# First head group's scores in float32 from raw q and k, its probabilities copied by VectorE, and seven expert matmuls in every unit

## The chip, the cores and the metric

The kernel runs on one core of a Trainium2 chip. The metric is the device time of one execution in microseconds (us). Five engines work side by side, each through its own list of instructions in order: TensorE (PE, matmuls and their weight loads), VectorE (DVE), ScalarE (ACT), GpSimd (POOL) and SyncE (SP), whose list here issues nearly all the DMAs. They wait for each other at semaphores. Matmul results land in PSUM, in eight banks.

## The reference, cut to what matters

Attention with a window of 128 positions and four sink positions for 2 batches, 8 heads, 768 positions and 64 dimensions; its output, 1536 rows of 512, goes through a mixture of 8 experts (hidden width 1024) and then through a dense layer pair (hidden width 2048).

```python
scores = scale * np.matmul(q, k.transpose(0, 1, 3, 2))
keep = is_sink | in_window
scores = np.where(keep, scores, -1e9)
a = np.exp(scores - max); a = a / (sum + 1e-9)
x = np.matmul(a, v)                  # then rows of 512
h = np.maximum(x @ w1[e], 0.0)       # for each expert e
out += P[:, e:e+1] * (h @ w2[e])     # P: balanced gate
```

## The kernel before

**Stages.** `phase_a` computes the attention and, in its gaps, the first chunk of the first expert; `phase_b` does the rest of that chunk and all other chunks. Most products are made in three fp32r passes: each operand is split into a high part (cast by ACT) and a low part (operand minus high part, by POOL or DVE), and the passes are low x high, high x low, high x high.

**Units.** The attention is cut into 4 head groups (batch and half of the sequence) of 4 head pairs each, and each pair `n` into three units `l`, one for 128 rows of queries. Unit `u = 3n + l`. The first group is u = 0 to 11 (n < HP = 4). The score block of a unit is 128, 256 or 288 columns wide in the first and third group (672 in all for a pair) and 288 in the others. Both heads of a pair stand in the two halves of the 128 partitions.

**The loop** (`phase_a`, one turn for each u) issues in this order: the scores of unit u + 2 (`att_qk`, PE); the exponential of unit u + 1 (`att_exp`, ACT); from the second group on the sum, reciprocal and normalisation of unit u (`att_sum`, `att_recip`, `att_norm`, DVE); the masked maximum of unit u + 2 (`att_max`, DVE); a part of `att_x` for the pair before (the output's high part on ACT, its low part `xl` on DVE or POOL); `evac()`, which empties the PSUM bank of every expert group that is complete; a number of steps of the filler; the transposes of unit u (`att_transpose`, PE) and their copy out of PSUM (`att_copy`, ACT: pT, and skT in units with l = 2); in units with l = 0 the product with v for the pair before (`att_av`, PE).

**The first group** is normalised late: `late_recip` builds reciprocals of the row sums and spreads them over 384 columns (DVE), `late_rows` transposes these (L300, PE) and copies them out (L301, DVE), and `att_x` multiplies the output with them (L393, DVE).

**The filler** steps through the 25 groups of `first_groups`, 12 matmuls each: for each of four blocks of 384 rows four groups of `mm1` (384 columns, L593) and three of `mm2` (512 columns, L618), the last three of `mm2` being issued by `phase_b`. A thirteenth step closes a group and opens the next. A block of rows may be worked on only when its attention is complete: `ready` is 0 up to u = 12, 1 up to u = 25, 2 up to u = 37, then 3. Each unit takes up to `MMS[l]` steps and stops at a group's end (`not self.done`). All these groups use the two banks of `ps_mm`. Scores of odd units of the first group use these banks too (`mmtile`).

**The loads.** `att_load_qk` issues q and k of a pair, `att_load_v` its v. The raw tile of pair n + 3 is loaded when that of n + 2 has been split, into the only buffer of `attraw` (pair 1 has a tile of its own among pT's).

**The end.** `phase_b` takes its weight tiles from the space that the attention gives back, loads the next chunk's weights, runs the filler to its end (with `units`, the splits of the next chunk's weights, between its groups) and then begins the next chunk (`plain`, L751).

Of the kernel before, what the change touches and what calls it, by code (L numbers as in the profile page):

```python
# [10 lines left out]
F32 = mybir.dt.float32  # L11
# [13 lines left out]
MMS = (4, 8, 8)  # L25
# [23 lines left out]
class Kernel:  # L49
# [119 lines left out]
    def att_load_qk(self, n, cut=None):  # L169
        g, hp = divmod(n, HP)  # L170
        b, half = divmod(g, 2)
        if n == 1:
            raw = self.attp.tile([128, 2 * S], F32, tag="pth", name="raw1")
        else:
            raw = self.attraw.tile([128, QKW[1]], F32, tag="raw", name="raw")
        cuts = [0, QKW[half]] if cut is None else [0, cut, QKW[half]]
        for i, j in zip(cuts, cuts[1:]):
            self.nc.sync.dma_start(out=raw[:, i:j], in_=self.qkv[half][b, hp][:, i:j])
        self.raw[n] = raw
# [10 lines left out]
    def att_split_qk(self, n, part):  # L190
        nc = self.nc
        half = (n // HP) % 2
        if part == 0:
            self.qk[n] = tuple(
                self.att2.tile([128, QKW[1]], F32R, tag="qk" + t, name="qk" + t) for t in "hl"
            )
        hi, lo = self.qk[n]
        raw = self.raw[n]
        if n == 0:

            def cut(t):
                if part == 3:
                    return t[:, 2 * QW : QKW[half]]
                t = t[:, 0 : 2 * QW].rearrange("p (j c) -> p j c", c=QW)
                return t[:, :, 128 * part : 128 * part + 128]

        else:
            m = QW + 256 if half == 0 else QW + WB

            def cut(t):  # L210
                return t[:, 0:m] if part == 0 else t[:, m : QKW[half]]

        nc.scalar.activation(out=cut(hi), in_=cut(raw), func=AF.Copy)  # L213
        nc.gpsimd.tensor_tensor(  # L214
            out=cut(lo), in0=cut(raw), in1=cut(hi.bitcast(F32)), op=ALU.subtract
        )
# [15 lines left out]
    def att_qk(self, u):  # L232
        nc = self.nc
        n, l, g, hp, half, off, wd, mask, tt = self.unit(u)
        hi, lo = self.qk[n]
# [4 lines left out]
        for a in range(2):  # L240
# [5 lines left out]
            for m, (x, y) in enumerate(((lo, hi), (hi, lo), (hi, hi))):  # L246
                nc.tensor.matmul(
                    out=ps[:, 0:wd],
                    lhsT=x[r, l * 128 : (l + 1) * 128],
                    rhs=y[r, QW + off : QW + off + wd],  # L250
                    start=(m == 0),
                    stop=(m == 2),
                )
# [93 lines left out]
    def att_copy(self, u):  # L347
# [4 lines left out]
        if l == 0:  # L352
            self.pT[n] = self.attp.tile([128, 2, 768], F32, tag="pth", name="pT")
        nc.scalar.activation(
            out=self.pT[n][:, :, o : o + w], in_=self.ptp.pop(u)[:, :, 0:w], func=AF.Copy
        )
        if l == 2:
            w = 128 if half == 0 else QW
            nc.scalar.activation(out=self.skT[0:64, 0:w], in_=self.skp[:, 0:w], func=AF.Copy)
# [673 lines left out]
    def run(self):  # L1033
# [18 lines left out]
        if True:  # L1052
            with tc.manual_schedule():
# [3 lines left out]
                with ExitStack() as actx:  # L1057
                    self.wraw = self.pool(actx, "wraw0")
                    self.att = self.pool(actx, "att")
                    self.attraw = self.pool(actx, "attraw")  # L1060
# [123 lines left out]
    def phase_a(self, gen):  # L1184
# [6 lines left out]
        for part in range(4):  # L1191
            self.att_split_qk(0, part)
        self.att_split_qk(1, 0)
# [9 lines left out]
        self.att_split_qk(1, 1)  # L1203
        self.att_load_qk(2)
        self.att_load_v(1)
        fill = self.filler(gen)
        at = next(fill)
        for u in range(U + 2):
# [9 lines left out]
            if u == 3 * HP - 1:  # L1218
                self.att_transpose(u)
                self.att_copy(u)  # L1220
# [12 lines left out]
            if l == 1 and n and not now:  # L1233
                steps = self.att_x(n - 1)
                next(steps, None)
            if l == 2 and 0 < n < HP:
                next(steps, None)
                next(steps, None)
            if late and l == 2:
                self.late_recip(n)  # L1240
            self.evac()
            if u < 3 * HP - 1:
# [4 lines left out]
            for _ in range(MMS[l]):  # L1247
                ready = 1 if 3 * HP < u < 6 * HP else (u - 2) // (3 * HP)
                if at is not None and at < ready * QW and not self.done:
# [10 lines left out]
            if l == 1 and n + 2 < N:  # L1260
# [235 lines left out]
```

## Time and profile before

| | us |
|---|---|
| median of 3 runs | 1396.65 (1395.65 to 1397.15) |
| profiled execution, its own time | 1395.19 |
| span of that execution, first to last instruction | 1393.0 |
| PE busy | 1369.5 |
| DVE busy | 948.7 |
| POOL busy | 512.9 |
| ACT busy | 462.4 |

How to read what follows: busy times are of one profiled execution. A row of the order of time begins with the start and the duration in us, then engine, line, operation, output <- input, the number of instructions merged in the row (xN) and, in brackets, how long the engine was idle before it and on what it had waited. A matmul in float32 appears as two instructions.

### The profile page before, as it was taken

What the parts mean: (1) busy time and instruction counts of PE and PEld (TensorE: products, weight loads), DVE (VectorE), ACT (ScalarE), POOL (GpSimd) and SP (SyncE); (2) the same over time, 40 slices, a digit from 0 to 9 for tenths busy, and PEclk for the clock granted to TensorE, in tenths of its full rate; (3) what the DMA queues carried; (4) which work ended last, traced back from release to release, by engine and by line L of the source; (5) the groups of instructions that cost most, each with busy time, mean ns of one, the idle gap of its engine ahead of it and who ended that gap; (6) DMA issues with size and microseconds to landing.
All of it is one profiled execution on the core that took longest, in us unless ns stands there. A gap on an engine that the chain in (4) does not pass through costs nothing.

```text
span 1393.0 us, 18988 instructions
## 1 busy us (share of the span) xinstructions
PE 1369.5 (98%) x7129; PEld 1148.4 (82%) x7129; DVE 948.7 (68%) x1868; ACT 462.4 (33%) x1033; POOL 512.9 (37%) x452
## 2 busy tenths in 40 slices
PE   7899999999999999999999999999999999999998
PEld 5566888888888888888888888888888888888887
DVE  5778348987867777777777777675454557876564
ACT  8767323322222222222222322222222234443331
POOL 6422116543432334244333434343333035543310
PEclk9999999999999999999999999999999999999999
DMA  5323200222223232322323132330102010211101
GB/s 168 97 87 91 76 15 17 76 68 95 80 91 106 76 106 66 109 84 91 105 63 121 54 121 69 106 106 32 61 31 61 31 57 5 76 44 63 46 24 71
DMA packets 61146, 102.53 MB, mean 74 GB/s; under 512 B 3956, under 2 KB 43252, under 8 KB 60788
## 3 DMA queue, kind: packets, MB, share of 16 engines
q1 hardware_dynamic: 61040, 101.22, 22.5%
q8 instruction: 58, 0.95, 0.3%
q14 instruction: 44, 0.36, 0.1%
q10 hardware_dynamic: 4, 0.00, 0.0%
HBM read 89.67 MB, written 11.53 MB: 73 GB/s over the span
## 4 chain that ended last, share of the span: by engine, by line
PE 78%; DVE 0%; issue 0%; DVEq 0%
PE mm L902 41%; PE mm L751 36%; PE mm L919 0%; DVE acc L642 0%; DVE acc L638 0%; DVE raw L567 0%; DVE tx L811 0%; DVE raw L554 0%; DVE tu L811 0%; DVE acc L635 0%; DVE raw L559 0%; DVE raw L563 0%; DVEq L642 0%; DVE m L571 0%; DVEq L811 0%
## 5 line engine op out<-in xcount | busy, mean ns | idle before, releaser
L902 PE MATMUL mm<-w2h,hh 128*128 128x512 f32 (+1 forms) x916 | 357.0, 390 | 0.0
L902 PE MATMUL mm<-w2l,hh 128*128 128x512 f32 (+1 forms) x916 | 355.9, 389 | 0.0
L902 PE MATMUL mm<-w2h,hl 128*128 128x512 f32 (+1 forms) x916 | 355.7, 388 | 0.0
L471 POOL TENSOR_TENSOR w2l<-raw,w2h 128x512 fp32r<-128x512 f32 x76 | 118.4, 1558 | 383.7 <-ACT w2h L470 381.8
L642 DVE SCALAR_TENSOR_TENSOR acc<-mm,P,acc 128x512 f32<-128x512 f32 x168 | 125.6, 748 | 135.5 <-PE mm L902 134.1
L902 PEld LDWEIGHTS mm<-w2h,hl 128*128 128x128 f32 x916 | 172.0, 188 | 35.8
L902 PEld LDWEIGHTS mm<-w2h,hh 128*128 128x128 f32 x916 | 172.1, 188 | 34.6
L902 PEld LDWEIGHTS mm<-w2l,hh 128*128 128x128 f32 x916 | 172.1, 188 | 34.4
L514 POOL TENSOR_TENSOR raw<-raw 128x256 f32<-128x256 f32 x136 | 125.8, 929 | 9.0 <-DMA raw<-w 1.1
L471 POOL TENSOR_TENSOR s0l<-raw,s0h 128x512 fp32r<-128x512 f32 (+1 forms) x36 | 45.5, 1265 | 199.0 <-ACT s0h L470 199.0
L719 ACT ACTIVATE hh<-tx 128x512 fp32r<-128x512 f32 (+1 forms) x112 | 58.9, 525 | 130.0 <-DVE tx L811 129.5
L811 DVE TENSOR_TENSOR tx<-mm,tu 128x512 f32<-128x512 f32 (+1 forms) x136 | 75.6, 556 | 21.5 <-PE mm L751 17.4
L811 DVE TENSOR_TENSOR tx<-mm,tx 128x512 f32<-128x512 f32 (+1 forms) x68 | 37.9, 557 | 57.0 <-PE mm L751 55.7
L729 DVE SCALAR_TENSOR_TENSOR hl<-tx,hh 128x512 fp32r<-128x512 f32 (+1 forms) x112 | 70.0, 625 | 9.8 <-ACT hh L719 9.8
L825 ACT ACTIVATE tx<-mm 128x512 f32<-128x512 f32 x34 | 20.4, 599 | 159.7 <-PE mm L751 157.8
L214 POOL TENSOR_TENSOR qkl<-raw,qkh 128x672 fp32r<-128x672 f32 (+5 forms) x34 | 42.7, 1279 | 74.2 <-ACT qkh L213 44.4
L635 DVE TENSOR_TENSOR acc<-mm,acc 128x512 f32<-128x512 f32 (+1 forms) x49 | 33.2, 677 | 50.9 <-PE mm L902 50.5
L719 ACT ACTIVATE hh<-mm 128x512 fp32r<-128x512 f32 (+1 forms) x68 | 34.2, 502 | 99.4 <-PE mm L751 99.4
L825 ACT ACTIVATE txs<-mm 128x256 f32<-128x256 f32 x34 | 13.0, 382 | 151.3 <-PE mm L751 151.3
L471 POOL TENSOR_TENSOR a0l<-raw,a0h 128x512 fp32r<-128x512 f32 (+1 forms) x38 | 43.8, 1171 | 51.1 <-ACT a0h L470 51.1
L751 PE MATMUL mm<-xl,a1h 128*128 128x512 f32 (+1 forms) x172 | 60.3, 350 | 0.0
L751 PE MATMUL mm<-xl,a0h 128*128 128x512 f32 (+1 forms) x172 | 59.8, 348 | 0.0
(262 smaller groups left out, 3202.8 us busy)
## 6 DMA issues: line engine op xcount, KB each, us to landing
raw<-w SPq DMA_DIRECT2D x110, 512.0 KB, 3.5
raw<-win SPq DMA_DIRECT2D x16, 512.0 KB, 4.0
w<-m SPq DMA_DIRECT2D x32, 256.0 KB, 4.7
raw<-wout SPq DMA_DIRECT2D x16, 512.0 KB, 4.1
raw<-qkv SPq DMA_DIRECT2D x8, 624.0 KB, 3.8
raw<-qkv SPq DMA_DIRECT2D x7, 464.0 KB, 3.4
out<-acc SPq DMA_DIRECT2D x11, 256.0 KB, 2.0
wraw<-w SPq DMA_DIRECT2D x2, 1024.0 KB, 6.5
```

The lines of the kernel that those rows point to most:

```text
L214: nc.gpsimd.tensor_tensor(out=cut(lo), in0=cut(raw), in1=cut(hi.bitcast(F32)), op=ALU.subtract)
L471: self.nc.gpsimd.tensor_tensor(out=lo, in0=src, in1=hi.bitcast(F32), op=ALU.subtract)
L514: self.nc.gpsimd.tensor_tensor(out=o, in0=x, in1=y, op=op)
L635: nc.vector.tensor_tensor(out=a, in0=ps, in1=a, op=ALU.add)
L642: nc.vector.scalar_tensor_tensor(out=a, in0=ps, scalar=self.P[:, ti, e : e + 1], in1=a, op0=ALU.mult, op1=ALU.add)
L719: nc.scalar.activation(out=hh, in_=src, func=AF.Relu)
L729: nc.vector.scalar_tensor_tensor(out=hl, in0=src, scalar=0.0, in1=hh.bitcast(F32), op0=ALU.max, op1=ALU.subtract,)
L751: self.nc.tensor.matmul(out=ps, lhsT=w[:, kc], rhs=x[:, kc], start=start and k == 0, stop=(k == n - 1), skip_group_check=True,)
L811: nc.vector.tensor_tensor(out=v[name], in0=v[a], in1=v[b], op=ALU.add)
L825: nc.scalar.activation(out=v["s"], in_=v["a"], func=AF.Copy)
L902: self.nc.tensor.matmul(out=ps[:, d], lhsT=x[:, f, s], rhs=w[:, f, d], start=(n == 0), stop=(n == 11),)
```

## The change

The first head group's scores are made in one float32 matmul for each head from the raw tiles, without a split of q and k; pairs 0 to 3 get raw tiles of their own, all issued at the start together with the load of pair 4, and `attraw` gets two buffers. In the first group `att_copy` runs on VectorE. `late_recip` moves ahead of the two `att_x` steps, and the transposes of unit 11 move back from before the exponential to their regular place. Each unit takes seven steps of the filler, whatever l, and goes on across a group's end.

```diff
-MMS = (4, 8, 8)
+MMS = 7
...
     def att_load_qk(self, n, cut=None):
-        if n == 1:
-            raw = self.attp.tile([128, 2 * S], F32, tag="pth", name="raw1")
+        if n < HP:
+            raw = self.att.tile([128, QKW[0]], F32, name=f"raw{n}")
...
     def att_qk(self, u):
-        hi, lo = self.qk[n]
+        if n < HP:
+            terms = ((self.raw[n],) * 2,)
+        else:
+            hi, lo = self.qk[n]
+            terms = (lo, hi), (hi, lo), (hi, hi)
...
-            for m, (x, y) in enumerate(((lo, hi), (hi, lo), (hi, hi))):
+            for m, (x, y) in enumerate(terms):
...
-                    stop=(m == 2),
+                    stop=(m == len(terms) - 1),
...
     def att_copy(self, u):
-        nc.scalar.activation(
-            out=self.pT[n][:, :, o : o + w], in_=self.ptp.pop(u)[:, :, 0:w], func=AF.Copy
-        )
+        jobs = [(self.pT[n][:, :, o : o + w], self.ptp.pop(u)[:, :, 0:w])]
         if l == 2:
             w = 128 if half == 0 else QW
-            nc.scalar.activation(out=self.skT[0:64, 0:w], in_=self.skp[:, 0:w], func=AF.Copy)
+            jobs.append((self.skT[0:64, 0:w], self.skp[:, 0:w]))
+        for out, src in jobs:
+            if n < HP:
+                nc.vector.tensor_copy(out=out, in_=src)
+            else:
+                nc.scalar.activation(out=out, in_=src, func=AF.Copy)
...
-                    self.attraw = self.pool(actx, "attraw")
+                    self.attraw = self.pool(actx, "attraw", 2)
...
     def phase_a(self, gen):
-        for part in range(4):
-            self.att_split_qk(0, part)
-        self.att_split_qk(1, 0)
...
         self.att_exp(0)
-        self.att_split_qk(1, 1)
         self.att_load_qk(2)
         self.att_load_v(1)
+        for n in (HP - 1, HP):
+            self.att_load_qk(n)
...
-            if u == 3 * HP - 1:
-                self.att_transpose(u)
-                self.att_copy(u)
...
+            if late and l == 2:
+                self.late_recip(n)
             if l == 2 and 0 < n < HP:
                 next(steps, None)
                 next(steps, None)
-            if late and l == 2:
-                self.late_recip(n)
             self.evac()
-            if u < 3 * HP - 1:
+            if late:
                 self.att_transpose(u)
                 self.att_copy(u)
...
-            for _ in range(MMS[l]):
+            for _ in range(MMS):
                 ready = 1 if 3 * HP < u < 6 * HP else (u - 2) // (3 * HP)
-                if at is not None and at < ready * QW and not self.done:
+                if at is not None and at < ready * QW:
                     at = next(fill, None)
...
-            if l == 1 and n + 2 < N:
+            if l == 1 and HP <= n + 2 < N:
                 self.att_split_qk(n + 2, 0)
                 self.att_split_qk(n + 2, 1)
```

## Rows read from the trace of the kernel before

**Rows 1.** The page, busy time of an engine and its share of the span
```profile
PE 1369.5 (98%) x7129; PEld 1148.4 (82%) x7129; DVE 948.7 (68%) x1868; ACT 462.4 (33%) x1033; POOL 512.9 (37%) x452
```

**Rows 2.** Stretches: length, busy time of each engine (instructions), granted clock, DMA
```profile
12.73:19.35 6.62, 6.62 (x55) 4.76 (x55) 4.06 (x20) 6.49 (x22) 4.75 (x5) 1.00 0.36 108
16.72:22.31 5.59, 5.36 (x50) 3.73 (x49) 3.73 (x17) 5.46 (x19) 4.21 (x4) 1.00 0.31 97
...
28.00:32.00 4.00, 4.00 (x27) 2.62 (x26) 0.69 (x2) 3.65 (x13) 3.48 (x3) 0.58 0.39 130
...
38.00:42.00 4.00, 3.97 (x24) 2.69 (x24) 3.44 (x17) 0.00 (x0) 0.00 (x0) 0.61 0.61 179
...
59.65:69.82 10.17, 8.88 (x65) 6.33 (x65) 9.08 (x42) 7.58 (x24) 3.43 (x3) 1.00 0.25 77
```

**Rows 3.** Waits of PE, 0 to 46 and 42 to 185: total, times, longest
```profile
PE mm L300 <- DVE acc L286: 3.2, 1, 3.2
PE ptp L331 <- ACT p L272: 2.1, 2, 1.9
...
PE ptp L331 <- DVE p L318: 6.4, 7, 1.3
```

**Rows 4.** Groups of ACT from 12.73 to 19.35: count, busy, mean ns
```profile
L354 ACT ACTIVATE pT<-ptp 128x512 f32<-128x512 f32 x2 | 1.2, 585 | 0.1
...
L213 ACT ACTIVATE qkh<-raw 128x288 fp32r<-128x288 f32 x2 | 0.9, 430 | 0.0
...
L213 ACT ACTIVATE qkh<-raw 128x640 fp32r<-128x640 f32 x1 | 0.7, 730 | 0.0
L354 ACT ACTIVATE pT<-ptp 128x256 f32<-128x256 f32 x1 | 0.4, 359 | 0.0
L359 ACT ACTIVATE skT<-skp 64x128 f32<-64x128 f32 x1 | 0.3, 254 | 0.0
```

**Rows 5.** Groups of DVE (L633: durations least, median, most in ns)
```profile
L633 DVE COPY acc<-mm x10: 682/690/692, 88.7 to 187.3; 128x512 f32<-128x512 f32 x10
...
L301 DVE COPY acc<-mm 128x384 f32<-128x384 f32 x1 | 0.6, 558 | 0.2 <-PE mm L300 0.2
...
L260 DVE CUSTOM_DVE_ANT_0 p<-sc,mb 128x288 f32<-128x288 f32 x2 | 0.8, 452 | 0.0
...
L318 DVE TENSOR_SCALAR_CACHE_REDUCE p<-p,st x70: 345/511/515, 41.9 to 146.1; 128x288 f32<-128x288 f32 x54, 128x128 f32<-128x128 f32 x8, 128x256 f32<-128x256 f32 x8
```

**Rows 6.** Order of time on PE, first stage
```profile
19.28 0.30 PE L247 MATMUL sc<-qkl,qkh 64*128 64x288 f32 x2
19.41 0.30 PE L247 MATMUL sc<-qkh 64*128 64x288 f32 x2
...
20.86 1.30 PE L377 MATMUL xp<-pT,vraw 128*64 128x256 f32 x12
...
38.03 0.55 PE L300 MATMUL mm<-ident,acc 128*128 128x128 f32 x3 [3.25 <-DVE acc L286]
...
44.97 0.41 PE L247 MATMUL sc<-qkh,qkl 64*128 64x288 f32 x2
```

**Rows 7.** Order of time on PE, a run of fill and the transposes behind it
```profile
57.42 0.44 PE L593 MATMUL mm<-xl,w0h 128*128 128x384 f32 x1
57.70 0.34 PE L593 MATMUL mm<-xh,w0h 128*128 128x384 f32 x1
...
58.05 0.33 PE L593 MATMUL mm<-xl,w0h 128*128 128x384 f32 x1
59.70 0.41 PE L331 MATMUL ptp<-ident,p 128*128 128x128 f32 x2 [1.31 <-DVE p L318]
```

**Rows 8.** Order of time, the end of the attention and of the drain
```profile
149.47 0.82 PE L377 MATMUL xp<-skT,vs 128*64 128x384 f32 x4
...
154.91 1.99 POOL L471 TENSOR_TENSOR a0l<-raw,a0h 128x512 fp32r<-128x512 f32 x2 [4.47 <-ACT a0h L470]
...
179.79 0.39 PE L751 MATMUL mm<-xl,a0h 128*128 128x512 f32 x1
```

## What the change will do to the time

> **What bounds the kernel now.** I read the page first, then the busy time by stretches, the waits of TensorE (PE), and last the order of time on each engine. Over the whole span of 1393.0 us PE is 98% busy [rows 1], but a busy share is a mean over stages, so the stages were looked at one by one. Three lie within the part that the change touches.
>
> *Stage 1*, 0 to 45 us, units 0 to 13: the attention of the first head group, with no expert matmul to fill gaps (the first that `ready` allows comes in unit 13). Here ScalarE (ACT) is the bound: in the 6.62 us of one head pair it is busy 6.49 [rows 2]. PE waits 1.9 us for an exponential and 3.2 us for the row sums of the pair before [rows 3]; behind each of these two idles the granted clock is 0.58 and 0.61 for about 4 us [rows 2], so that PE works there partly at 1.2 instead of 2.4 GHz.
>
> *Stage 2*, units 14 to 49, up to the last attention matmul at 150.3 (149.47 plus 0.82) [rows 8]: PE is the bound, except for seven waits, 6.4 us, of the transposes for VectorE's (DVE's) normalisation [rows 3]. Each wait stands in a unit with l = 0, behind its four fill matmuls; the row of 59.70 is one of them [rows 7].
>
> *Stage 3*, the drain: with quotas 4, 8, 8 and a stop at each group end, a group of 12 matmuls needs 13 steps of the generator, so l = 0 gives four, l = 1 eight, l = 2 only the closing step. One group in three units; 13 of 25 are placed by unit 49. The rest runs back to back until the next expert begins at 179.79 [rows 8]. From there on nothing is changed, PE is dense, and whatever arrives earlier ends earlier.
>
> **The change, stage 1.** ACT loses, per pair, two copies of 0.585, one of 0.36 and one of 0.25, in sum 1.78 us, and the casts of pairs 0 to 3, 0.73 and two of 0.43 (those of two neighbouring pairs stand in the stretch), 1.59 us [rows 4]. 6.49 - 3.37 leaves 3.1; pairs 2 and 3 keep casts of later pairs, about 1.3, so 4.4. ACT is no bound any more. GpSimd (POOL) loses its subtractions.
>
> DVE gets the copies. A copy from PSUM of 128x512 took it 0.69, one of 128x384 0.558 [rows 5]; by that slope 128x256 takes 0.42 and the small one 0.29. Per pair 2 x 0.69 + 0.42 + 0.29 = 2.09, on top of 3.73 [rows 2]: 5.8 us.
>
> PE: three fp32r passes become one float32 matmul. A score pass of 288 columns, both heads side by side, takes 0.13 us (19.28 to 19.41), 0.45 ns a column. How fast a float32 matmul is shows in the product with v: 12 instructions for six matmuls, so two each, 1280 columns for each head, both heads side by side, in 1.30 us [rows 6]; less a tail of 0.15 this is 0.9 ns per column and instruction. A float32 score column thus costs 1.8 instead of 1.35 ns; with 672 columns a pair that is 0.3 us more. Bounds: nothing (the fixed part around three passes shrinks), and 1.5 us if the two heads, in different rows of the array here and not in different columns, do not run side by side (672 x (3.6 - 1.35)). I take 0.3, because the three passes did run side by side in the same rows. PE then has 5.36 + 0.3 = 5.7 us a pair.
>
> So DVE and PE stand level, each in order, and they cross twice in a pair: the row transposes (L300) need DVE's `late_recip`, and the product with v needs the last copy and `skT`. Walking the two queues through a pair, I find about 0.2 us of wait at each crossing beyond what the one queue's lead covers, together 0.35, so 6.05 us a pair.
>
> The start changes little: the first maximum (`att_max(0)`) waits for the masks that DVE builds, which no part of the change touches; later starts gain about 0.5 us from the freed ACT. Then two pairs at 6.05 (scores of units 6 and 9; the first begins at 16.72) bring the score of unit 12. From there DVE sets the time up to the score of unit 16. Its list, with the steps of 384 columns at the 0.558 of L301: four maxima, each two rows of 0.452 that overlap by 0.07, 3.0; the copies of units 10 and 11, 1.6; two products with the row factors, two `xl` and the row copy, 2.8; `late_recip`, 0.75 with its reciprocal; two normalisations, each two rows of 0.511 and some 0.45 of sums and reciprocal, 2.95 [rows 5]. That is 11.1, and 0.9 until its first score is there: 12.0. Before, the way from 16.72 to the score of unit 16 at 44.97 [rows 6] took 28.25; now 2 x 6.05 + 12.0 = 24.1. With the 0.5 the gain is **4.65 us**. In it lies the moved `late_recip`: it now stands ahead of the `xl` step, which waits for ACT, so that the wait of 3.25 before the row transposes [rows 6] goes; what is late next is the copy of unit 11, and behind it the normalisation of unit 12. Bounds: 0 (DVE is held at each crossing and a pair takes 7 us again) and 8.5 (PE dense at 5.7 a pair, 6.6 behind it).
>
> The waits that are added: DVE's copy waits for PE's transposes, with the next maximum queued behind it, and for that maximum waits the exponential of the next unit but one; this is in the walk. The DMAs of raw3 and raw4 are issued early, behind v1 on SP's queue; nothing that is needed before unit 7 stands behind them.
>
> **Stages 2 and 3.** Seven steps in each unit make 91 in units 13 to 25, exactly the seven groups that `ready` allows, and 168 later: 19 groups and 12 matmuls of the next. Some seven groups leave the drain for stage 2. The PE work is the same; what is won is waits. The wait at 59.70 lasts in truth from 58.05 + 0.17 to 59.70, 1.48 us where 1.31 is listed [rows 7], because ends are modelled; seven of them with 0.17 each on top give 7.6. Where there were four matmuls there are seven (0.5 us more cover), and a pair's three units become 1.6 to 2.1 us longer while DVE's work grows by 0.4; DVE had 9.08 us of work in the 10.17 of its fullest pair, the one with `general_flag` [rows 2], so it comes early. I let 0.2 remain. Bounds: 3.6 (only the 0.5 of cover each) and 8.
>
> Added is one more run of fill a pair, in l = 2, 12 in all. The first matmul of a run takes 0.28 to the next (57.42 to 57.70) instead of 0.17 (57.70 to 58.05 for two) [rows 7]; 0.11 x 12 is 1.3 us; since the transposes behind a run lose some of their own start, I take half, 0.7. Bounds 0 and 1.3. Sum: 7.6 - 0.2 - 0.7 = **6.7 us**.
>
> Against this stands a rule of the Trainium skill, TensorEngine Tiling (Array Packing), Key Properties: a change of the tiling mode drains TensorE, and score, fill and transpose have different tiles. By it a run pays on entry and on exit; at 0.11 on either side that is 2.6 us in all, and the time would be about 1387. The trace shows the 0.11 on entry; on exit no row shows it alone.
>
> Cover at the end: after the last attention matmul the weights of the next expert are loaded, cast and subtracted, until 156.9 for the first half (154.91 plus 1.99) [rows 8], 6.6 us after 150.3. Left for that time are 7 + 12 matmuls of 512 columns, 0.23 each by the 0.17 for 384, and 48 of 384: 12.5 us. They hide it at no cost. Without that cover each us missing costs a us.
>
> Two banks for the groups: the group that begins within a unit takes the bank of the group before last, which ended at least one `evac()` ago. So nothing.
>
> **Sum.** The profiled execution took 1395.19 (span 1393.0 and 2.2 around it): 1395.19 - 4.65 - 6.7 = 1383.8. The median of the three runs is 1.46 above it; I predict **1385.3**.
>
> **Rivals.** (a) *VectorE takes the place of ScalarE.* For: 5.8 us beside PE's 5.7, in order. If it is held at each crossing, or float32 scores run one after the other, stage 1 gains 0 to 1; if also the transposes of l = 0 still wait, 3.6 less 0.7 to 1.3 there. With one or both, 2.3 to 8 us are won: 1388.5 to 1394.5. Against: DVE had 1.9 us a pair without work before (3.73 of 5.59 [rows 2]).
> (b) *More is won.* Without the two idles the clock stays up, PE sets the pace: 8.5 + 7.5 = 16: 1380.5. Against: DVE's list of 11.1 us in a row.
> (c) *Slower: two banks are too few.* The stop at a group's end is gone; if the new group's first matmul must wait until the unit's `evac()` has emptied a bank, it waits for DVE's copy of 0.69 and one row of the maxima ahead of it, 0.38 [rows 5]: 1.07 us at 20 ends, 21 lost and 11.35 won: 1406.5. It decides from 0.57 us an end. Against: the order of banks above.
> (d) *The fill does not get in*: if `ready` or an empty generator stops it, stage 2 gains nothing, and 1392 remains. The count of 91 speaks against it.
>
> **How the numbers follow.** Forecast with its bounds (1381.5 to 1388.5): 0.62. (a) 0.21, (b) 0.08, (c) 0.05, (d) and other mishaps that end near no change 0.04. 0.2% is 2.8 us, about what a measurement of this kernel tells from no change. Faster: 0.62 + 0.08 + 0.18 of (a) = 0.88; same 0.03 of (a) + 0.04 = 0.07; slower 0.05. The range from 1379.5 to 1391.5 leaves out (c), (d) and the ends of (a) and (b), under 0.2.
>
> **What would show it.** Score of unit 16 at about 40.3 instead of 44.97; ACT under 75% and DVE about 95% busy between 16 and 28; float32 score rows of about 0.5 us for 288 columns, two side by side; no PE wait over 0.5 for L318 behind unit 14; the next expert's first matmul near 168.5 instead of 179.79, without a wait for its weights. Wrong would be: PE waiting in fill rows for `hl` or `acc` (c), or for DVE's copies in stage 1 (a).

## The result and the profile after

The changed kernel takes 1379.32 us (median of 4 runs, 1378.92 to 1380.15), the kernel before, in the same session, 1396.22 (1395.65 to 1397.15): a ratio of 0.9879, 95% interval 0.9862 to 0.9896. It is faster by 16.9 us, where 11.35 had been forecast, and it lies 0.2 us below the low end of the range. The profiled execution took 1378.92, with a span of 1377.1; before it was 1395.19 and 1393.0, so the two profiles differ by 16.3 us (15.9 in the span), and it is these that the steps below account for.

The page of the kernel after, its line of busy times (engine, us, share of the span, instructions), against [rows 1]:

```profile
PE 1363.8 (99%) x7105; PEld 1142.8 (83%) x7105; DVE 953.6 (69%) x1884; ACT 453.8 (33%) x1007; POOL 501.8 (36%) x442
```

PE's busy time fell by only 5.7 us, a third of the gain; most of it is idle time that went. Stretches of the kernel after in stage 1 (length, busy time of each engine with its instructions, granted clock, DMA), against [rows 2]:

```profile
20.00:30.00 10.00, 10.00 (x80) 6.85 (x79) 9.23 (x36) 8.75 (x28) 7.04 (x6) 1.00 0.38 103
30.00:40.00 10.00, 9.37 (x62) 6.49 (x60) 9.54 (x43) 5.78 (x17) 2.39 (x3) 1.00 0.78 279
```

PE is without a gap from 20 to 30, DVE stands close behind it with 9.23, and in the next ten microseconds DVE is the fuller one (9.54 against 9.37). The stretches with a granted clock of 0.58 and 0.61 [rows 2] are gone: the clock is 1.00 in both, and from 38 to 42 as well. Of the signs that the prediction named, ACT was busy for 9.71 and DVE for 10.76 of the 12 us from 16 to 28, 81% and 90%, where under 75% and about 95% had been named.

Waits of PE after the change, first from 0 to 46 us, then from 36 to 180 (total, times, longest), against [rows 3]:

```profile
PE mm L126 <- DVE nw_f L121: 4.1, 1, 4.1
PE sc L242 <- DVE st L255: 0.9, 2, 0.5
PE mm L295 <- DVE acc L281: 0.3, 1, 0.3
...
PE mm L591 <- DVE hl L603: 0.4, 1, 0.4
PE mm L616 <- ACT hh L602: 0.4, 1, 0.4
...
PE ptp L326 <- DVE p L313: 0.3, 1, 0.3
```

The wait of 4.1 lies at the very start and is there in every kernel here (3.7 to 4.2 us). The two large waits of stage 1 (3.2 and 1.9) went to 0.3 and nothing; the seven of the transposes for the normalisation (6.4) became one of 0.3. The first two rows of the second window are waits of fill for the emptying of a group that has ended, which the forecast had put at nothing: 0.8 us as listed. The first is for the group's bank, which is free when `hl` has been written; the second is of `mm2` for `hh`, the values that the emptying makes.

The order of time on PE after the change, against [rows 6] and [rows 8] (start, duration, engine, line, operation, instructions, and in brackets the idle time before the row):

```profile
15.75 0.59 PE L242 MATMUL sc<-raw 64*128 64x128 f32 x4
...
18.19 0.76 PE L242 MATMUL sc<-raw 64*128 64x288 f32 x4
18.88 0.44 PE L326 MATMUL ptp<-ident,p 128*128 128x128 f32 x2
...
21.54 0.90 PE L242 MATMUL mm<-raw 64*128 64x128 f32 x4
...
27.26 0.40 PE L242 MATMUL sc<-qkh,qkl 64*128 64x288 f32 x1
...
38.34 0.37 PE L242 MATMUL sc<-qkh,qkl 64*128 64x288 f32 x1 [0.39 <-DVE st L255]
...
150.03 0.82 PE L375 MATMUL xp<-skT,vs 128*64 128x384 f32 x4
163.58 0.39 PE L749 MATMUL mm<-xl,a0h 128*128 128x512 f32 x1
```

The scores of units 6, 9, 12 and 16 begin at 15.75, 21.54, 27.26 and 38.34; before, the first and the last of these were at 16.72 and 44.97 [rows 6]. The next expert begins at 163.58 instead of 179.79 [rows 8], with no wait for its weights. Of the 16.2 us between these two, 6.6 are won up to the score of unit 16 and 9.6 behind it (163.58 - 38.34 = 125.24 us, before 134.82).

### The profile page after: what moved, and what is told of

It is laid out like the page before. It is cut to its first block, busy times and chain, and to the rows that moved or that the text cites. A ratio compares the mean times of both kernels' runs of the same rounds, so it can differ in the third digit from the quotient of the medians.

```text
span 1377.1 us, 18909 instructions
## 1 busy us (share of the span) xinstructions
PE 1363.8 (99%) x7105; PEld 1142.8 (83%) x7105; DVE 953.6 (69%) x1884; ACT 453.8 (33%) x1007; POOL 501.8 (36%) x442
## 4 chain that ended last, share of the span: by engine, by line
PE 79%; DVE 1%; ACT 0%; issue 0%; DVEq 0%; ACTq 0%
PE mm L900 42%; PE mm L749 36%; PE mm L917 0%; ACT tx L720 0%; DVE acc L640 0%; DVE tx L721 0%; ACT hh L732 0%; DVE tx L809 0%; DVE hl L733 0%; DVE acc L636 0%; DVE mm L721 0%; DVE raw L565 0%; ACT tx L823 0%; DVE raw L552 0%; DVE tu L809 0%
## 5 line engine op out<-in xcount | busy, mean ns | idle before, releaser
L633 DVE TENSOR_TENSOR acc<-mm,acc 128x512 f32<-128x512 f32 (+1 forms) x49 | 33.2, 677 | 50.8 <-PE mm L900 50.5
L749 PE MATMUL mm<-xh,a0h 128*128 128x512 f32 (+1 forms) x172 | 59.8, 347 | 0.0
```

What stands on the lines that cost most here:

```text
L633: nc.vector.tensor_tensor(out=a, in0=ps, in1=a, op=ALU.add)
L749: self.nc.tensor.matmul(out=ps, lhsT=w[:, kc], rhs=x[:, kc], start=start and k == 0, stop=(k == n - 1), skip_group_check=True,)
```

## Experiments

Two questions stood at the start: whether the two halves of the change, stage 1 and the fill, give what the steps of the sum say, and which part of each half does it. In each diff a line with a minus is that of the kernel named in the sentence ahead of it.

### The fill alone, and the change without it

The kernel before with the new fill only:

```diff
-MMS = (4, 8, 8)
+MMS = (7, 7, 7)
...
-                if at is not None and at < ready * QW and not self.done:
+                if at is not None and at < ready * QW:
```

> The kernel before with only the new fill: seven steps in each unit, across group ends. Theory A (the first stage won 6.5 us, the fill 9.7: beside the listed waits, PE also lost time inside rows of its scores, where the second head began late): about 9.7 us below the kernel before, 1386.5. Theory B (the fill won the 6.7 us of the prediction, and the first stage more than its own clock of 6.5 tells): 1389.5.

Measured: 1386.13 us (1385.49 to 1387.38), ratio 0.9924 (0.9907 to 0.9940); the span is 8.4 us shorter. Its waits of PE from 36 to 185:

```profile
PE mm L300 <- DVE acc L286: 4.6, 1, 4.6
...
PE ptp L331 <- DVE p L318: 0.3, 1, 0.3
```

The seven waits are gone here too, and the score of unit 16 to the next expert takes 46.07 to 171.49, 125.4 us, as in the kernel after (125.2). So all of the gain in stages 2 and 3 is the fill's. Its span gains less than the 9.4 us of that stretch because its own stage 1 ended 1.1 us later in this execution (46.07 for 44.97; the wait of L300 is 4.6 where it was 3.2).

The kernel after with the old fill:

```diff
-MMS = 7
+MMS = (4, 8, 8)
...
-            for _ in range(MMS):
+            for _ in range(MMS[l]):
...
-                if at is not None and at < ready * QW:
+                if at is not None and at < ready * QW and not self.done:
```

> The changed kernel with the old fill (4, 8, 8 steps, stop at a group's end): the first stage alone. Theory A: 6.5 us below the kernel before, 1389.7. Theory B: 9.5 us below, 1386.7.

Measured: 1389.07 us (1388.68 to 1389.59), ratio 0.9945 (0.9929 to 0.9962), span 6.2 us shorter. The score of unit 16 is at 38.71 and the next expert at 173.15, 134.4 us between them, as before. The waits of the transposes are back:

```profile
PE ptp L326 <- DVE p L313: 5.5, 6, 1.3
```

Theory A, written down with the traces of before and after already read, holds in both runs, by the times and by the stretches (9.4 us and 6.3). The halves are nearly separate: 8.4 and 6.2 us of the spans make 14.6, and the whole change 15.9; most of the 1.3 between is the late stage 1 of the first run.

### Spreading the old amount of fill

The kernel before with its 13 steps a pair in equal parts, across group ends, so that no unit is without fill but none is much longer:

```diff
-MMS = (4, 8, 8)
+MMS = (5, 4, 4)
...
-                if at is not None and at < ready * QW and not self.done:
+                if at is not None and at < ready * QW:
```

> The kernel before with the old amount of fill (13 steps in three units, one group) spread evenly: 5, 4, 4 steps, across group ends. If the waits came from the units without any fill (PE ahead of VectorE in scores, transposes and the next unit's normalisation), spreading alone wins most of what the new fill wins: 6 to 9 us, 1388 to 1391. If the amount is what counts (PE has too little work for VectorE's 7.4 to 9 us a pair), the waits only move to other units: 0 to 3 us, 1394 to 1397.

Measured: 1390.14 us (1389.49 to 1390.99), ratio 0.9945 (0.9926 to 0.9964), span 5.3 us shorter, as the forecast for waits from units without fill had it. From the score of unit 16 on it wins 4.6 us of the 9.4 that the fill of seven wins (table below), so the amount counts as much as the spreading. The listed waits of the transposes fell from 6.4 us to 0.7:

```profile
PE ptp L331 <- DVE p L318: 0.7, 3, 0.3
```

With nearly the same short list of waits, the fill of seven has a span 3.1 us shorter and is 4.8 us better from the score of unit 16 on. Where these lie is seen by taking PE's order of time apart into blocks (a block runs from the start of its first matmul to the start of the next block, so a wait counts to the block before it), from the score of unit 16 to the first matmul of the next expert:

| us | before | 5, 4, 4 across ends | 7 on before | after |
|---|---|---|---|---|
| scores (32 blocks) | 21.18 | 20.88 | 18.56 | 18.89 |
| transposes | 23.18 | 23.43 | 20.52 | 20.20 |
| fill, up to the transposes behind it | 67.89 | 63.33 | 63.75 | 63.58 |
| products with v | 22.57 | 22.56 | 22.59 | 22.57 |
| sum | 134.82 | 130.20 | 125.42 | 125.24 |
| runs of fill | 25 | 36 | 36 | 36 |
| score blocks of 0.80 or more | 10 | 8 | 0 | 1 |
| transpose blocks of 0.80 or more | 8 | 12 | 3 | 2 |

The fill blocks fall by 4.3 to 4.6 us as soon as the fill is spread, and more fill adds nothing there. The other 5.3 us, in scores and transposes, come only with seven steps. The order of time on PE of the kernel before shows the two kinds of score block:

```profile
128.34 0.41 PE L247 MATMUL sc<-qkh,qkl 64*128 64x288 f32 x2
...
128.94 0.66 PE L331 MATMUL ptp<-ident,p 128*128 128x128 f32 x4
...
129.64 0.40 PE L247 MATMUL sc<-qkh,qkl 64*128 64x288 f32 x1
...
129.95 0.40 PE L247 MATMUL sc<-qkh,qkl 64*128 64x288 f32 x1
...
130.53 0.44 PE L593 MATMUL mm<-xl,w0h 128*128 128x384 f32 x1
```

and, of the same kernel, one row of the weight loads (PEld) and one of DVE:

```profile
129.64 0.18 PEld L247 LDWEIGHTS sc<-qkh,qkl 64*128 64x128 f32 x1 [0.20 <-DVE st L260]
...
129.43 0.45 DVE L260 CUSTOM_DVE_ANT_0 p<-sc,mb 128x288 f32<-128x288 f32 x1
```

At 128.34 the two heads start together (x2), and the block lasts 0.60, to 128.94. At 129.64 the first head starts alone and the second 0.31 later, and the block lasts 0.89. PE is busy throughout, so this is a wait that no list shows. What the second head waits for is the maximum of the unit before, which DVE makes head by head and which frees the bank: the weight load of the first head is released by DVE's `st`, the maximum of the second head runs from 129.43 and has been read out by 129.89, and the second head's matmul follows at 129.95. It is the same in all ten slow score blocks of this kernel: the second head starts 0.05 to 0.07 us after the end of that maximum, which falls 0.18 to 0.25 us behind the start of the block; in the 22 others both maxima had ended at least 0.4 us before the block began. For the transposes, too, the weight loads of the kernel before name the wait:

```profile
60.16 0.20 PEld L331 LDWEIGHTS ptp<-ident,p 128*128 128x128 f32 x2 [0.29 <-DVE p L318]
```

This is inside the block that begins at 59.70 [rows 7]. Having waited for the first head's normalisation, the transposes wait a second time, for the second head's, and PE's modelled ends cover that: the row of 59.70 reads on as busy. There are six such blocks before, with 0.29 each, and four of narrow units with 0.19 (blocks of 0.56 instead of 0.31). With seven steps DVE is ahead in all but two places and the blocks are of 0.64, as this one of the kernel after:

```profile
42.92 0.60 PE L326 MATMUL ptp<-ident,p 128*128 128x128 f32 x4
...
43.56 1.52 PE L375 MATMUL xp<-pT,vraw 128*64 128x128 f32 x16
```

About 0.5 of the 3.0 us that the transposes win is no wait: ten of their blocks stood directly behind scores, where nine of them took 0.69 to 0.70, and behind a run of fill they take 0.64.

### Eight steps, and an earlier emptying of the banks

The kernel after with one step more in each unit:

```diff
-MMS = 7
+MMS = 8
```

> The changed kernel with eight steps in each unit: the 21 groups that ready allows are all placed by unit 49, the four groups that remain, 8.3 us, cover the 6.6 us until the next expert's weights. PE is dense from unit 14 on but for some 3 us of waits: 0 to 1 us won, 1378.3 to 1379.3. If the cover fails, each us missing shows as a wait of the first matmul of the next expert: 1380 to 1383.

Measured: 1386.33 us (1386.26 to 1386.91), ratio to before 0.9916 (0.9887 to 0.9946): 7.0 us slower than with seven, and neither forecast had it. Its waits of PE from 36 to 185, and one of them in the order of time with what ACT and DVE did ahead of it:

```profile
PE mm L591 <- DVE hl L603: 4.5, 3, 2.5
PE mm L616 <- ACT hh L602: 1.4, 2, 1.0
PE mm L616 <- DVE acc L631: 0.5, 2, 0.3
```

```profile
50.27 0.34 PE L591 MATMUL mm<-xh,w0l 128*128 128x384 f32 x1
53.07 0.44 PE L591 MATMUL mm<-xl,w0h 128*128 128x384 f32 x1 [2.46 <-DVE hl L603]
...
49.17 1.33 ACT L204 ACTIVATE qkh<-raw 128x672 fp32r<-128x672 f32 x2
50.40 0.62 ACT L418 ACTIVATE w1h<-wraw 128x512 fp32r<-128x512 f32 x1
...
51.96 0.47 ACT L602 ACTIVATE hh<-mm 128x384 fp32r<-128x384 f32 x1
...
52.46 0.56 DVE L603 SCALAR_TENSOR_TENSOR hl<-mm,hh 128x384 fp32r<-128x384 f32 x1 [2.22 <-ACT hh L602]
```

The rows for `hl` and `acc` are rival (c), two banks too few, one step beyond the change; that for `hh` is `mm2` waiting for the values of a group that is emptied late. A group ended in the run of fill before; its emptying is issued in this unit and queues on ACT behind two casts of 1.33 us together, one of 0.62 and the exponentials. The other bank's group ends at 50.27, and the group that follows it in the same unit wants the bank that ACT and DVE only release at 53.0. With seven steps for groups of thirteen a group ends in about every second unit and the emptying has a unit's time; with eight, ends come in neighbouring units more often. That ends come in neighbouring units is worked out from the counts and was not tested by itself. The waits come to 6.4 us; besides, the granted clock is 0.61 from 53 to 57, behind the idle of 2.46. The next expert begins at 171.54, again with no wait for its weights.

The emptying moved to the head of the unit, in the kernel after and in that with eight steps:

```diff
             late = n < HP
+            self.evac()
             now = u == 3 * HP + 1
...
-            self.evac()
             if late:
                 self.att_transpose(u)
```

> The changed kernel with evac() at the start of a unit, behind its scores, instead of behind its maxima. If the remaining waits in the fill (0.4 for hl, 0.4 for hh) are evacuations queued behind exponentials, normalisation and maxima: they go, 0.5 to 1.5 us won, 1378 to 1379. If the normalisation, now 0.56 later, makes the transposes wait instead: 1379.5 to 1382.

> Eight steps in each unit with evac() at the start of a unit. If the 7 us that eight steps cost are waits for banks and for hh and hl, which are emptied too late in the unit: most of them go, 1379 to 1381. If they are something else (the cover at the end, ready): they stay, 1385 to 1386.5.

Measured: with seven steps 1394.04 us (1389.64 to 1395.25 in ten runs, and the profiled one, 1395.25, is the slowest of them), 14.7 slower than the kernel after; with eight 1386.50 (1385.46 to 1388.06), no better than eight alone. Waits of PE from 36 to 185 with seven:

```profile
PE ptp L326 <- DVE p L313: 9.5, 8, 2.2
```

With eight the same wait comes to 3.4 us in seven places, and that of fill for `hl` falls from 4.5 to 1.6.

Both forecasts for seven steps had it near the kernel after and were wrong; the second named the right wait, at a small part of its size. With eight the time is the one named for "they stay", but for another reason: the waits in the fill do shrink, and those of the transposes take their place. With seven the waits in the fill do go, but DVE's share of the emptying, `hl`, now stands ahead of the sums and the normalisation in DVE's queue, and it waits there for ACT. The kernel with seven steps and early emptying, one such place on DVE and what came of it on PE:

```profile
44.16 0.56 DVE L603 SCALAR_TENSOR_TENSOR hl<-mm,hh 128x384 fp32r<-128x384 f32 x1 [2.33 <-ACT hh L602]
...
45.69 0.90 PE L326 MATMUL ptp<-ident,p 128*128 128x128 f32 x4 [1.47 <-DVE p L313]
```

The 2.33 us that DVE stands still hold up the normalisation behind it, and with it the transposes. So of the two places tried the old one, behind the maximum, is the better.

### The parts of stage 1

The kernel after with the copies of the first group on ScalarE, as before:

```diff
-            if n < HP:
-                nc.vector.tensor_copy(out=out, in_=src)
-            else:
-                nc.scalar.activation(out=out, in_=src, func=AF.Copy)
+            nc.scalar.activation(out=out, in_=src, func=AF.Copy)
```

> The changed kernel with the copies of the first group's probabilities back on ScalarE. If VectorE's list sets the time between the scores of units 12 and 16, as the prediction has it: 1.6 us of copies go from it, 1377.7, and the two pairs before keep their 5.75 us. If ScalarE becomes the bound again (3.1 + 1.8 + 1.3 = 6.2 us a pair with the casts of the next group): 0.5 us a pair longer and the last copies behind its exponentials, 1380.5 to 1382.

The kernel after with `late_recip` behind the two steps of `att_x`, as before:

```diff
-            if late and l == 2:
-                self.late_recip(n)
             if l == 2 and 0 < n < HP:
                 next(steps, None)
                 next(steps, None)
+            if late and l == 2:
+                self.late_recip(n)
```

> The changed kernel with late_recip back behind the two att_x steps. If its place alone made the wait of 3.25 us before the row transposes of pair 3: 2 to 3 us of that wait return, 1381.5. If ScalarE's load made it (its xh came late), late_recip now only waits for one xl of 0.55 us: 0 to 0.5 us, 1379.3 to 1379.8.

Measured: 1379.71 us (1379.00 to 1380.07) and 1378.98 (1378.13 to 1380.02), beside 1379.32 for the kernel after; the span is 1377.1 in all three. Neither part alone matters. For `late_recip` the second forecast came out, for the copies neither did. With the copies on ACT, DVE has time but waits for ACT, and the product with v of the last late pair, which needs the bank that `xl` reads, waits in turn. The kernel after with the copies on ACT, one row of DVE and one of PE:

```profile
32.43 0.56 DVE L395 TENSOR_TENSOR xl<-xp,xh 128x384 fp32r<-128x384 f32 x1 [1.49 <-ACT xh L392]
...
33.04 1.30 PE L372 MATMUL xp<-pT,vraw 128*64 128x256 f32 x12 [1.50 <-DVE xl L395]
```

Its score of unit 16 is at 38.54, beside 38.34: what ACT takes from DVE's list it gives back as a wait.

Then the parts by themselves. Float32 scores alone, with the raw tiles and the second buffer of `attraw` that go with them: the kernel after with the old fill, the copies on ACT, `late_recip` behind, and unit 11's transposes early as in the kernel before; and the same with unit 11's transposes in their regular place. Against the kernel with the old fill above, the first is:

```diff
-            if n < HP:
-                nc.vector.tensor_copy(out=out, in_=src)
-            else:
-                nc.scalar.activation(out=out, in_=src, func=AF.Copy)
+            nc.scalar.activation(out=out, in_=src, func=AF.Copy)
...
+            if u == 3 * HP - 1:
+                self.att_transpose(u)
+                self.att_copy(u)
...
-            if late and l == 2:
-                self.late_recip(n)
             if l == 2 and 0 < n < HP:
                 next(steps, None)
                 next(steps, None)
+            if late and l == 2:
+                self.late_recip(n)
...
-            if late:
+            if u < 3 * HP - 1:
                 self.att_transpose(u)
```

> Of the first stage's edits the raw float32 scores alone (with their tiles and loads); copies on ScalarE, late_recip and the transposes of unit 11 as before, old fill. If the splits were the whole of it: as with all edits of the first stage, 1389. If the copies or the order have a part that shows only here: 1391 to 1394.

and the second, against the first:

```diff
-            if u == 3 * HP - 1:
-                self.att_transpose(u)
-                self.att_copy(u)
...
-            if u < 3 * HP - 1:
+            if late:
                 self.att_transpose(u)
```

> The kernel with the raw float32 scores alone, old fill, and the transposes and copies of unit 11 in their regular place (copies still on ScalarE, late_recip still behind the two att_x steps). If the early place of unit 11's copies, ahead of the exponential of unit 12 and of xh on ScalarE, made the wait of 3.4 us before the row transposes: that wait falls under 1.5 and the time is that of all first-stage edits, 1389 to 1390. If it needs the copies on VectorE or the late_recip ahead: the wait stays at 3 and the time at 1392.

And the copies alone, the kernel before with `att_copy` of the first group on VectorE:

```diff
-        nc.scalar.activation(
-            out=self.pT[n][:, :, o : o + w], in_=self.ptp.pop(u)[:, :, 0:w], func=AF.Copy
-        )
+        jobs = [(self.pT[n][:, :, o : o + w], self.ptp.pop(u)[:, :, 0:w])]
         if l == 2:
             w = 128 if half == 0 else QW
-            nc.scalar.activation(out=self.skT[0:64, 0:w], in_=self.skp[:, 0:w], func=AF.Copy)
+            jobs.append((self.skT[0:64, 0:w], self.skp[:, 0:w]))
+        for out, src in jobs:
+            if n < HP:
+                nc.vector.tensor_copy(out=out, in_=src)
+            else:
+                nc.scalar.activation(out=out, in_=src, func=AF.Copy)
```

> The kernel before with the first group's copies on VectorE and nothing else. If ScalarE's load of 6.5 us a pair is the cause, 1.8 us off it serves as the casts do: 4 to 6 us won, 1391 to 1393. If the path through cast and subtraction to the scores (POOL) is the cause, the wait before the row transposes stays: 0 to 2 us, 1395 to 1397.

Measured: float32 scores alone 1392.32 us (1391.07 to 1394.22), ratio 0.9964 (0.9949 to 0.9980); with unit 11 in its place 1391.20 (1390.54 to 1393.00), 0.9957 (0.9940 to 0.9974); copies alone 1396.63 (1393.87 to 1397.68), 0.9990 (0.9978 to 1.0003), which can't be told from no change. With the medians as they are, the scores and their tiles carry 4.6 to 5.4 us of the 8.2 of all of stage 1's parts (1396.9 less 1392.3, 1396.6 less 1391.2, 1397.3 less 1389.1). By the traces, one execution each, the score of unit 16 begins at 41.94 and 41.31, beside 38.71 with all of stage 1's parts and 44.97 before: 3.0 and 3.7 us of 6.3. All of that is won ahead of the score of unit 12: in the start, which scatters (unit 6 at 15.43 and 15.55, before 16.72), and in the two pairs behind it, which take 11.39 and 11.26 us instead of 13.91. From there to the score of unit 16 they need 15.12 and 14.50, no less than the 14.34 of before, and all the parts together 10.98. What is missing there is the wait for the row sums, which stays, with a low clock behind it; for the second kernel the forecast that it would stay came nearer (2.8 us, with unit 11 early 3.4). The kernel with float32 scores and unit 11 in its place, one row of PE, two of DVE and two stretches:

```profile
33.28 0.90 PE L295 MATMUL mm<-ident,acc 128*128 128x128 f32 x3 [2.77 <-DVE acc L281]
...
31.97 0.56 DVE L395 TENSOR_TENSOR xl<-xp,xh 128x384 fp32r<-128x384 f32 x1 [2.18 <-ACT xh L392]
32.45 0.18 DVE L280 RECIPROCAL acc<-acc 128x6 f32<-128x6 f32 x1
```

```profile
34.00:38.00 4.00, 4.00 (x22) 2.55 (x21) 2.87 (x14) 0.00 (x0) 0.00 (x0) 0.50 0.41 132
38.00:42.00 4.00, 4.00 (x27) 3.20 (x26) 3.49 (x16) 2.70 (x8) 0.00 (x0) 0.85 0.73 224
```

DVE's `late_recip` (32.45) stands behind `xl`, which waits 2.18 for ACT's `xh`. It is enough to free ACT of the copies, so that `xh` comes early, or to put `late_recip` ahead of `xl`: with either one the wait is 0.8 or less, with neither it is 2.8 to 3.4. That is why each looked like nothing when it alone was undone.

The copies without float32 scores win nothing for another reason. ACT is not full in that kernel (8.53 of the 12 us from 16 to 28, before 11.17); its queue stands still for loads. Waits of the issue of loads (SPq) and one row of ACT, the kernel before with the copies on VectorE:

```profile
SPq L178 <- POOL qkl L214: 14.2, 4, 3.9
```

```profile
33.37 1.34 ACT L213 ACTIVATE qkh<-raw 128x672 fp32r<-128x672 f32 x2 [2.46 <-DMA raw<-qkv]
```

The single buffer of `attraw` goes round from the load (3.4 to 3.8 us to landing) to ACT's cast and POOL's subtraction (2.3 to 3.0 us), and only then is the next load issued: the casts begin at 18.62, 25.61 and 33.37, 7.0 and 7.8 apart, and ACT waits 5.9 us for `raw` in three places, with `xh` queued behind the last of them. Before, where the casts begin 7.1 and 7.8 apart, ACT waits 0.9 there. So in stage 1 the way round this buffer was about as long as ACT's work, and the change takes away both at once. What raw tiles of their own and a second buffer would win with the split scores, no run here tells.

## Why the prediction was right in direction and too small

The profiled execution was to take 1383.8 and took 1378.92, 4.9 us less. The predicted median stood 1.46 above that, as before's did; after's stands 0.40 above, another 1.1. The kernel before scatters more: seven of its executions in one session took 1394.86 to 1399.38 with a mean granted clock of 0.997 to 0.994, the four of the kernel after 1378.92 to 1380.15 with 0.999.

| step | predicted | measured |
|---|---|---|
| start, to the score of unit 6 | gain 0.5 | gain 0.97 |
| one late pair | 6.05 | 5.79, 5.72 |
| score of unit 12 to that of unit 16 | 12.0 | 11.08 |
| stage 1, gain | 4.65 | 6.63 |
| fill blocks, gain (waits less run starts) | 6.7 | 4.3 |
| scores and transposes of stage 2, gain | 0 | 2.3 + 3.0 |
| stages 2 and 3, gain | 6.7 | 9.6 |

**What bounds the kernel** was read rightly in the main: in stage 1 ACT and two waits, though the single raw buffer, which was not named, held the pairs about as tightly; in stage 2 the transposes' wait for DVE, and everything won before the next expert is kept. Both halves gave a gain of their own, and the weights at the end stayed hidden.

**The float32 score.** Predicted about 0.5 us for 288 columns of both heads side by side and 0.3 more for a pair. Measured 0.69 from start to start (18.19 to 18.88), where three passes of this width take 0.60 (128.34 to 128.94); with 0.63 instead of 0.55 for 256 columns and 0.52 instead of 0.49 for 128 it is 0.2 us a pair. Where both heads of the narrow block start together (copies on ACT) it takes 0.42, and the sum is 0.1. The heads do run side by side; the price was on the near end of its bounds.

**A pair.** 6.05 was forecast and 5.79 and 5.72 measured, but not by the terms of the sum. With the copies on ACT, and with float32 scores alone, the first of the two pairs takes 5.31, so PE's own work is no more than that, 0.4 less than the 5.7 of the prediction. The crossings with DVE then cost 0.4 to 0.5, more than the 0.35 that had been put down: 0.3 of it at L295 in the first pair, and in the second pair no wait is listed, but the heads of the score at 21.54 start 0.21 apart and its block takes 0.83. So the nearness of 5.7 to the measured pair is luck.

**The last part of stage 1.** DVE sets it, as predicted: PE waits for DVE's `st` at 38.34. But its list was 11.1 long by adding durations and is 10.3 in the trace (from its first maximum at 28.07 to 38.34), because neighbouring rows overlap; with 0.8 ahead of it that is 11.08. The subtraction was made for the maxima alone. The 0.47 more at the start can't be told from scatter: in single executions of kernels that do the same up to there, the score of unit 6 lies between 15.75 and 16.86 with the change (five kernels), and between 15.92 and 17.27 without it (three).

**Stages 2 and 3: the step that failed** is "the PE work is the same; what is won is waits", taken with the seven listed waits as the whole of them. It is 2.9 of the 4.9 us; the other 2.0 are the three rows of stage 1. The waits that were not in the list were worth about 4.7 us, those of the second head in scores and transposes, inside rows that read as busy; with the 0.5 of the transposes that no longer stand behind scores this is the 5.3 that the sum had at nothing. The fill's own part came out smaller, 4.3 in its blocks. The 7.6 us of the seven waits were sized about rightly (from the last fill matmul to the transposes these places took 8.76 us, 7.2 to 7.6 more than 0.17 to 0.23 each), but "two banks, so nothing" failed: a group emptied late holds the fill twice, listed with 0.4 each, and from start to start 0.76 instead of 0.17 (at 51.72) and 0.81 instead of 0.23 (at 63.24), 1.2 us. The 11 new runs cost 0.11 each, 1.2 in these blocks; the half that the prediction took off stands in the row of the transposes, as the 0.5 there. The two errors offset each other in part. The cause that the prediction named, longer units that let DVE come early, is right, and is the one that brings the waits of the second head: 13 steps a pair spread evenly leave most of them, 21 remove nearly all.

**The drain of the array.** By the rule of the Trainium skill (TensorEngine Tiling (Array Packing), Key Properties) that a change of tiling mode drains TensorE, a run pays on both sides, 2.6 us in all by the prediction's working. The entry from the scores is there, 0.28 for the first matmul of a run, as before. The prediction read the other side wrongly: in its own rows fill and transposes have the same tile, `128*128` [rows 7], and of the three only the scores have another, `64*128` [rows 6], so by the rule nothing is due between fill and transposes. The trace agrees: transposes and `skp` take 0.64 behind a run of fill (42.92 to 43.56) and 0.70 behind scores (128.94 to 129.64, before). A run between scores and transposes thus costs 0.11 on entry and saves 0.05 behind it, about 0.7 us for the 11, which is what the prediction took.

**The rivals.** (a) DVE as the bound: for the last 11 us of stage 1 it is, and this was in the sum; elsewhere PE sets the pace. (b) Nearest in time (1380.5), and its reason about stage 1 was half right: no half clock any more, pairs near PE's pace, but DVE's list held in the last part; what was won beyond the forecast lay mostly in stage 2, so the nearness is luck in part. Its 8.5 us, the upper bound of stage 1, doesn't come out of the terms beside it either: 28.25 less 2 x 5.7 less 6.6 is 10.25, and 10.75 with the 0.5 of the start. (c) Late emptying costs 1.2 us here and most of 7 with one step more; the order of the banks was the right argument, with less in hand than it sounded. (d) The fill got in.

## What to carry to other kernels

A row of waits counts only idle time. Where ends are modelled and two heads wait one after the other, compare the start-to-start time of the same kind of block in good and bad places, and take the sum of the differences as what can be won. Filler work should be spread so that each unit is long enough for the engine that feeds it, but every step more must be held against the banks: of the fills tried here seven was best and eight lost 7 us. A part that looks idle when it alone is undone may be one of two that do the same thing. And a full engine may share its place with a buffer that goes round at the same pace: taking work off the engine then wins nothing until the buffer is freed as well.

## What the runs showed of the hardware

**The clock behind idles.** In the kernel after, PE idles at most 0.5 us at a time between 6 and 36 us, and the granted clock stays at 1.00. With the copies on ACT an idle of 1.50 leaves 1.00 as well. Behind the idle of 2.77 in the kernel with float32 scores and unit 11 in its place (the stretches above) it is 0.50, the level of 1.2 GHz, over four microseconds and 0.85 over the next four; behind 1.9 it was 0.58 [rows 2, 3]. Early emptying of the banks made this matter in stage 2, its stretches:

```profile
54.00:58.00 4.00, 2.54 (x12) 1.86 (x13) 3.79 (x20) 2.53 (x9) 2.65 (x3) 0.81 0.00 0
58.00:62.00 4.00, 4.00 (x29) 3.35 (x30) 1.27 (x7) 1.91 (x7) 0.00 (x0) 0.77 0.02 4
```

Behind the wait of 1.47 at 45.69 the clock is 1.00 (stretch 46 to 50), behind one of 2.18 (at 55.41) 0.81 and 0.77. Such a wait costs more than it lasts, which is a part of the 14.7 us that this version lost beside 9.5 us of listed waits.

The length of the idle does not settle it. In the kernel before, the wait of 1.31 at 59.70 left the clock at 1.00 [rows 2, 7]; in the kernel with float32 scores and unit 11 in its place the same wait did not:

```profile
56.04 1.15 PE L326 MATMUL ptp<-ident,p 128*128 128x128 f32 x4 [1.31 <-DVE p L313]
```

```profile
56.00:60.00 4.00, 3.96 (x23) 2.51 (x25) 3.04 (x14) 2.84 (x10) 1.11 (x1) 0.57 0.02 4
```

With float32 scores alone an idle of 1.32 at 56.66 is followed by a low clock too, while in the fill on the kernel before an idle of 2.04 at 27.90 left it at 1.00. From the score of unit 16 to the next expert the two kernels of float32 scores took 136.2 and 136.3 us, where the kernel before, with the same waits listed there (seven, 6.4 us) and the clock at 1.00, took 134.8: such a fall cost some 1.4 us in these executions. Which of the idles it strikes, no run here explains.

**The first 14 us.** Rows of PE at the start last twice as long as later ones although the granted clock of their stretch reads 1.00; the kernel after:

```profile
6.76 1.53 PE L242 MATMUL sc<-raw 64*128 64x288 f32 x4 [0.49 <-DVE st L255]
8.23 0.69 PE L326 MATMUL ptp<-ident,p 128*128 128x128 f32 x2
```

```profile
8.00:10.00 2.00, 2.00 (x10) 1.22 (x9) 1.86 (x10) 1.81 (x7) 0.00 (x0) 1.00 1.05 389
```

The same score takes 1.47 us from start to start here (6.76 to 8.23) and 0.69 at 18.19. Either the granted clock isn't recorded yet at that time or something else halves the pace; no run here tells which.
